# Two token pairs of the first unit turned by VectorE and block transfers instead of TensorE, and three score groups placed behind value products

## The chip, the cores and the metric

One Trainium2 chip, one core. The metric is the device time of one execution in microseconds (us). The core's five engines each work through their own list in program order: PE (TensorE, matrix products), DVE (VectorE), ACT (ScalarE), POOL (GpSimd) and SP (SyncE, which here only issues DMA transfers). An instruction whose inputs aren't ready holds up all that stands behind it on its engine.

## The reference

For 8 batches, 8 heads, 576 tokens and a head width of 64, attention runs within chunks of 64 tokens; its output, with the heads side by side, is 4,608 tokens of 512 features. A normalised two-layer network with 2,048 hidden features follows, and its input is added back.

```
scores = scale * np.matmul(q_c, k_c.transpose(0, 1, 2, 4, 3))
attn = np.exp(scores - np.max(scores, axis=-1, keepdims=True))
attn = attn / (np.sum(attn, axis=-1, keepdims=True) + 1e-09)
x = np.matmul(attn, v_c)
...
xn = (x - mu) / np.sqrt(var + 1e-06) * g_ln
return x + np.maximum(xn @ w_ch1, 0.0) @ w_ch2
```

All of it is in float32 and close to exact: for the two layers each number is split into a high and a low part.

## The kernel before, in words

The 4,608 tokens are 18 pairs of 256 tokens ("pair" in the code), two pairs to a tile. The first three tiles (the lead, pairs 0 to 5) go through the two layers directly: `ffn`, with the products into the hidden features on L589 ("up") and those out of them on L613 ("down"), twelve 128x512 products each, three for each term because of the high and low parts. The other six tiles are three units of two tiles (pairs 6 to 9 are unit 0), whose two layers are computed by a recursive scheme with fewer products (`unit_ffn`, L1109, and `double`, L1039). That scheme needs the normalised tokens with features on the partitions, in a tile `rows`, which `combine` reads (L826 scales, L811 casts, L815 low parts, L818 differences).

`attention` is a generator for one pair: each `yield` ends a step. Its steps for a pair of unit 0 are: load queries and keys (`qk`, L294); the scores (L326); maxima (L333) and the load of the values (`v_t`, L344); subtraction (L359); exponential (L362); turning the probabilities, on PE (L376) or by DVE (L398, 16 instructions); sums; value products (L427); normalisation by the sums (L453 or L461); statistics (L471 to L480) and a copy of the pair to HBM (L274); a pause; the normalised tokens `xg` (L493, two on ACT); and last the tokens are turned so that features lie on partitions. In unit 0 that last part is, for the pairs 6, 8 and 9, eight PE transposes with the identity (L521) in two steps, each with an ACT copy (L522) into `rows`, and for pair 7 sixteen DVE transposes (L529). For pairs 10 and later ("moved") it is one DVE instruction, which turns all 32x32 blocks in place (L500), and then sixteen DMAs of 32 KB in four steps that carry the blocks to their partitions (L508).

The order of the work around here is written by hand. While tiles 1 and 2 go through `ffn`, the tables `SECOND` and `THIRD` say for each token of the `ffn`'s list which streams take a step ahead of it. The letters used below: A and B are pairs 4 and 5, C is pair 6, G is pair 7, D is pair 8, H is pair 9, P is `combine(0, 0)` (of pairs 6 and 8), and S is `prepare`. `prepare` makes weights for the units: POOL sums (L700 to L711), an ACT cast into the tile `parts` (L720), a POOL difference into the same tile (L722), and DMAs to HBM: `w2d` (L705), the four of `parts` (L713, issued one round later) and three of `wa` (L714 to L716). `parts` has one buffer, so the cast of a round waits until the four L713 transfers of the round before have landed. `a`, `b`, T, U and V are `mix` streams (L1077, L1084, ACT cast L1088, L1091, DMA L1093). ACT also makes the hidden features (L602), whose low part is made by DVE (L603).

All DMAs named here but the weights' accumulating ones are issued by SP, in program order, and their completion is counted on eight semaphores in turn, so that a DMA isn't issued before the one eight places ahead of it has landed.

Of the kernel before, what the change touches and what calls it, by code (L numbers as in the profile page):

```python
# [17 lines left out]
P = 128  # L18
B, H, S, D = 8, 8, 576, 64
# [7 lines left out]
NK = DM // P  # L27
# [8 lines left out]
LEAD = 3  # L36
UNITS = (NTILE - LEAD) // 2

SECOND = {
    0: "ABS", 1: "AS", 2: "S", 3: "AAS", 4: "AS", 5: "AS", 6: "AS", 7: "AS", 8: "AAS", 9: "AAS", 10: "AAS", 11: "BAS",  # L40
    12: "BACS", 13: "BS", 14: "S", 15: "BBS", 16: "BS", 17: "BS", 18: "BS", 19: "BS", 20: "BBCS", 21: "BBS", 22: "BBDS",
    23: "BCS", 24: "BCS", 25: "CS", 26: "S", 27: "CCS", 28: "CS", 29: "CCS", 30: "CDS", 31: "CDDS", 32: "DS",
}
THIRD = {
    0: "CS", 1: "CS", 2: "DDGS", 3: "DSaaaaa", 4: "aaaDDS", 5: "DS", 6: "DGS", 7: "GGHSbb", 8: "DGbb", 9: "Db",
    10: "bbTTGGP", 11: "TTHGGPb", 12: "G", 13: "GT", 14: "TTGGHPUU", 15: "GHPTUU", 16: "GHP", 17: "UGP",
    18: "UUHHGPVV", 19: "UHGPVV", 20: "HGPc", 21: "HHPV", 22: "HPVV", 23: "Vd", 24: "ccH", 25: "ccH", 26: "cQQ",
    27: "ccQR", 28: "cQ", 29: "QXXN", 30: "QQR", 31: "Q",
}
# [16 lines left out]
SINGLE = 6  # L66

BY_PE = 2

BY_DMA = (2, 3, 4, 5, 6, 7, 8, 9, 10)  # L70

# [30 lines left out]
def quad(i):  # L102
    return slice(32 * i, 32 * i + 32)
# [3 lines left out]
def chunk_attention_ffn(ctx: ExitStack, tc: tile.TileContext, qkv, v01, g, g_col, w, out):  # L107
# [34 lines left out]
    def weights(f):  # L142
        if f not in wp:
            wp[f] = const.tile([P, 2, NW], F32R, name="wp", tag=f"w{f}")
        return wp[f][:, 0, :], wp[f][:, 1, :]
# [59 lines left out]
    def split_w(i):  # L205
        wf = stage.pop(i)
        f, cs = part(i)
        wh, wl = (x[:, cs] for x in weights(f))
        if i < BY_PE:
            for j in range(wf.shape[1] // HALF):  # L210
# [70 lines left out]
    def attention(pair, xt_cols, xs, by_pe, den_by_pe, rows_of=None, pt_raw=False, pt_by_pe=False):  # L281

        moved = pair >= 2 * LEAD + 4
# [36 lines left out]
        for j in range(2):  # L320
            for a in range(HP):
                for h2 in range(2):
                    r = slice(h2 * D, (h2 + 1) * D)
                    for c in range(2):
                        cs = slice(j * P + c * D, j * P + (c + 1) * D)
# [46 lines left out]
        if by_pe:  # L372
            pt = halves()
            for a in range(groups):
                cs = slice(a % HP * P, (a % HP + 1) * P)
# [6 lines left out]
        elif pt_by_pe:  # L382
            pt = halves()
            for a in range(groups):
                cs = slice(a % HP * P, (a % HP + 1) * P)
# [34 lines left out]
        for j in range(2):  # L420
            for a in range(HP):
                for h2 in range(2):
                    r = slice(h2 * D, (h2 + 1) * D)
                    ja = j * HP + a
                    for c in range(2):
                        cs = slice(c * D, (c + 1) * D)
# [68 lines left out]
                )  # L495
            yield

        if rows_of and moved:
            turned = keep.tile([P, 4, 2 * NK, 32], F32, name="x")
            nc.vector.transpose(  # L500
                out=turned.rearrange("p b a t -> p a b t"),
                in_=xg.rearrange("p j (k b f) -> p (j k) b f", k=NK, b=4),
            )
            yield
            rows_t = rows_of().rearrange("p j k t -> p (j k t)").rearrange("p (j i n) -> p j i n", j=2, i=4)
            for i in range(4):
                for b in range(4):
                    nc.sync.dma_start(  # L508
                        rows_t[quad(b), :, i], turned[quad(i), b].rearrange("p (j k) t -> p j (k t)", j=2)
                    )  # L510
                yield
            return
# [260 lines left out]
    def start_ring():  # L773
        t_ = const.tile([P, 2, 2 * DM], F32R, name="ring", tag="w7")
        ring.add(t_[:, 0], t_[:, 1])
        yield
        for c in "hl":
            t_ = xtp.tile([P, 2, 2 * DM], F32R, name="ring", tag=f"xt{c}")
            ring.add(t_[:, 0], t_[:, 1])
        yield  # L780

    shared = {}

    def rows_of(i):
        if "rows" not in shared:
            shared["rows"] = [xtp.tile([P, 2, 2, NK, P], F32, name="rows", tag=f"xt{c}") for c in "hl"]
        return shared["rows"][i // 2][:, i % 2]

    def operand(name):
        if name not in shared:  # L790
            shared[name] = const.tile([P, 2, 2, 2 * PAIR], F32R, name="xc", tag=f"w{'3621457'.index(name)}")
        return shared[name]

    def combine(u, half=None):
        cs = slice(0, 2 * PAIR) if u > 0 else slice(half * PAIR, (half + 1) * PAIR)
        if u > 0:
            a, b = (
                r.rearrange("p i j k t -> p (i j k t)").rearrange("p (j k t) -> p k j t", k=NK, t=32)
                for r in shared["rows"]
            )  # L800
        else:
            a, b = (r[:, half].rearrange("p j k t -> p k j t") for r in shared["rows"])
        b11, b21, b12, b22 = a[:, :2], a[:, 2:], b[:, :2], b[:, 2:]

        def place(name):
            return operand(name)[:, :, :, cs].rearrange("p h k (j t) -> p h k j t", t=32 if u > 0 else P)

        engine = nc.vector if u > 0 else nc.gpsimd

        def cast(name, x):  # L810
            nc.scalar.copy(place(name)[:, 0], x)  # L811

        def low(name, x):
            o = place(name)
            engine.tensor_tensor(out=o[:, 1], in0=x, in1=o[:, 0].bitcast(F32), op=ALU.subtract)  # L815

        def less(out, x, y):
            nc.vector.tensor_tensor(out=out, in0=x, in1=y, op=ALU.subtract)  # L818

        def part(name, x):  # L820
            cast(name, x)
            low(name, x)

        def gain(x, first):
            for k in range(2):
                nc.scalar.activation(x[:, k], x[:, k], AF.Copy, scale=g_k[:, first + k : first + k + 1])  # L826

        if u > 0:
            steps = [
                [(gain, b21, 2), (gain, b11, 0)], [(cast, "2", b21), (gain, b12, 0)],  # L830
                [(low, "2", b21), (cast, "1", b11), (gain, b22, 2)], [(low, "1", b11), (cast, "3", b22)],
                [(less, b11, b12, b11)], [(low, "3", b22)], [(less, b12, b22, b12)], [(less, b22, b22, b11)],
                [(cast, "6", b22), (cast, "5", b11)], [(low, "6", b22)], [(less, b21, b21, b22)],
                [(low, "5", b11)], [(cast, "7", b12), (cast, "4", b21)], [(low, "7", b12)], [(low, "4", b21)],
            ]
        else:
            steps = [
                [(gain, b21, 2), (part, "2", b21), (gain, b11, 0)], [(part, "1", b11), (gain, b12, 0), (gain, b22, 2)],
                [(less, b11, b12, b11)], [(less, b12, b22, b12)],
                [(part, "3", b22)], [(less, b22, b22, b11)], [(part, "6", b22)], [(part, "5", b11)],  # L840
                [(less, b21, b21, b22)], [(part, "7", b12)], [(part, "4", b21)],
            ]
        for step in steps:
            for what, *args in step:
                what(*args)
            yield
# [219 lines left out]
    def mix(p, engine, pool, tag, again=False):  # L1066
        both = pool.tile([P, 2, 2, DM], F32, name="mixed", tag=tag)
        his, t_ = ([both[:, i, k] for k in range(2)] for i in range(2))
        if again:
            blocks = [[his[k], t_[k]] for k in range(2)]  # L1070
            for k in range(2):
                nc.sync.dma_start(both[:, :, k], w2d[2 * p + k])
            yield
        else:
            blocks = [[x[:, DM:].bitcast(F32) for x in weights(2 * p + k)] for k in range(2)]
        for k in range(2):
            engine.tensor_tensor(out=t_[k], in0=blocks[k][0], in1=blocks[k][1], op=ALU.add)  # L1077
            yield
        b11, b12, b21, b22 = (t_[k // 2][:, k % 2 * PAIR : (k % 2 + 1) * PAIR] for k in range(4))
        for k, (out, x, y, op) in enumerate((  # L1080
            (b11, b12, b11, ALU.subtract), (b12, b22, b12, ALU.subtract), (b22, b11, b22, ALU.subtract),
            (b21, b21, b22, ALU.add),
        )):
            engine.tensor_tensor(out=out, in0=x, in1=y, op=op)  # L1084
            if k % 2:
                yield
        for k in range(2):
            nc.scalar.copy(his[k].bitcast(F32R), t_[k])  # L1088
        yield
        for k in range(2):  # L1090
            engine.tensor_tensor(out=t_[k].bitcast(F32R), in0=t_[k], in1=his[k], op=ALU.subtract)  # L1091
            yield
        nc.sync.dma_start(wb[:, p], both.rearrange("p h k (a n) -> p h (k a) n", a=2))  # L1093
        yield
# [152 lines left out]
    with tc.manual_schedule():  # L1247
# [4 lines left out]
            G=tiles[3].attention(1), H=tiles[4].attention(1, True, pt_raw=True), S=prepare(), R=start_ring(), T=mix(4, nc.gpsimd, const, "w4"),  # L1252
            U=mix(5, nc.gpsimd, raws, "raw"), V=mix(6, nc.gpsimd, const, "w8"), a=mix(1, nc.vector, const, "w0"),
            b=mix(2, nc.gpsimd, const, "w1"), c=mix(0, nc.vector, const, "w9", True), d=mix(3, nc.gpsimd, const, "w10", True),
# [69 lines left out]
```

## Time and profile before

| | us |
|---|---|
| three runs, median (lowest, highest) | 819.19 (818.3, 820.9) |
| the profiled execution | 818.67 |
| its span, first to last instruction | 816.9 |
| PE busy in the span | 806.0 (99%) |
| DVE, ACT, POOL busy | 609.6, 363.1, 183.0 |

The profile is one execution. Its span begins with the first instruction of the program and ends with the last; 1.8 us of the execution's time lie around it. A row of the timeline gives the start, the length, the engine, the line, the operation, what it writes and reads, how many instructions are merged in it, and in brackets the idle time before it with what ended it. Consecutive products overlap in PE's pipeline, so what a group costs is read from the starts: from its first start to the first start of the next group. "SPq" is SP issuing a DMA; the length is that of the issue, not of the transfer. The answer for a line or a tile ends with the time from issue to landing.

### The profile page before, as it was taken

To read this page: it belongs to the slowest core of one execution; us is meant where nothing else is said; L and a number is where in the kernel's file an instruction comes from. 1 tells how busy PE (TensorE), PEld (TensorE's weight loads), DVE (VectorE), ACT (ScalarE), POOL (GpSimd) and SP (SyncE) were. 2 spreads that over 40 slices of the span, in tenths; PEclk is the share of its full clock that TensorE was granted. 3 is DMA by queue.
4 is the path that set the end of the run, shared out by engine and by line. 5 is a ranking of instruction groups with operands and counts; after the bars stand their busy time and mean duration, and the time that the engine had idled before them with its cause. 6 is when DMAs were issued, how large, how long until landed. Compare 5 with 4: busy or idle time off the path is not lost.

```text
span 816.9 us, 15499 instructions
## 1 busy us (share of the span) xinstructions
PE 806.0 (99%) x6170; PEld 680.3 (83%) x6170; DVE 609.6 (75%) x885; ACT 363.1 (44%) x545; POOL 183.0 (22%) x199
## 2 busy tenths in 40 slices
PE   7999999999999999999999999999999999999998
PEld 4888888888888888888888898888888988888887
DVE  6999975787665876869789987697799922249974
ACT  4776432121335434344567442443675522345450
POOL 0111005653857975610100001300000040000000
PEclk9999999999999999999999999999999999999999
DMA  9998315967786239988789578877796678668663
GB/s 359 331 291 243 156 52 183 364 201 253 272 307 252 104 129 367 368 300 302 250 248 329 184 236 307 278 276 257 239 334 213 183 236 252 186 203 285 193 214 108
DMA packets 113928, 201.06 MB, mean 246 GB/s; under 512 B 8512, under 2 KB 75072, under 8 KB 109888
## 3 DMA queue, kind: packets, MB, share of 16 engines
q1 hardware_dynamic: 112560, 195.35, 70.2%
q0 software_dynamic: 1296, 4.72, 3.0%
q8 instruction: 49, 0.80, 0.4%
q14 instruction: 23, 0.19, 0.1%
HBM read 142.89 MB, written 48.23 MB: 234 GB/s over the span
## 4 chain that ended last, share of the span: by engine, by line
PE 98%; DMA 1%; DVE 0%; issue 0%; SPq 0%; ACT 0%
PE y L1109 28%; PE h L589 16%; PE y L613 16%; PE y L1039 12%; PE h L1039 10%; PE s L1039 7%; PE s L326 2%; PE h L427 1%; DMA qk<-qkv 1%; PE s L427 1%; PE s L376 1%; PE s L353 0%; PE s L386 0%; PE y L251 0%; PE s L521 0%; PE y L542 0%
## 5 line engine op out<-in xcount | busy, mean ns | idle before, releaser
L1109 PE MATMUL y<-xc,ring 128*128 128x512 f32 x1008 | 233.4, 391 | 0.0
L1109 PEld LDWEIGHTS y<-xc,ring 128*128 128x128 f32 x1008 | 188.0, 188 | 39.5 <-issue 0.4
L613 PE MATMUL y<-wp,hidden 128*128 128x512 f32 x564 | 137.8, 393 | 0.0
L589 PE MATMUL h<-xth,wp 128*128 128x512 f32 (+1 forms) x432 | 129.6, 371 | 0.0
L613 PEld LDWEIGHTS y<-wp,hidden 128*128 128x128 f32 x564 | 104.4, 188 | 21.4
L1118 DVE TENSOR_TENSOR hu<-y,snap 128x512 f32<-128x512 f32 x72 | 49.2, 685 | 78.7 <-ACT snap L1115 38.3
L589 PEld LDWEIGHTS h<-xth,wp 128*128 128x128 f32 x432 | 78.2, 188 | 14.6 <-DVE hidden L603 0.6
L1039 PE MATMUL y<-ring,hx 128*128 128x512 f32 (+1 forms) x448 | 79.8, 337 | 0.0
L1115 ACT COPY snap<-y 128x512 f32<-128x512 f32 x72 | 41.8, 587 | 83.9 <-PE y L1109 83.8
L935 ACT ACTIVATE hx<-hu 128x1024 fp32r<-128x1024 f32 x61 | 64.3, 1061 | 33.0 <-PE h L1039 24.3
L589 PE MATMUL h<-xtl,wp 128*128 128x512 f32 (+1 forms) x216 | 78.3, 367 | 0.0
L1039 PEld LDWEIGHTS y<-ring,hx 128*128 128x128 f32 x448 | 69.6, 190 | 9.4
L603 DVE SCALAR_TENSOR_TENSOR hidden<-h,hidden 128x512 fp32r<-128x512 f32 (+1 forms) x53 | 33.0, 629 | 54.2 <-ACT hidden L602 54.0
L1039 PE MATMUL h<-ring,hx 128*128 128x256 f32 (+1 forms) x332 | 71.5, 319 | 0.0
L602 ACT ACTIVATE hidden<-h 128x512 fp32r<-128x512 f32 (+1 forms) x53 | 28.5, 545 | 95.5 <-PE h L589 95.5
L944 DVE TENSOR_TENSOR hx<-hu,hx 128x1024 fp32r<-128x1024 f32 x51 | 62.4, 1223 | 7.9 <-ACT hx L935 7.8
L1039 PE MATMUL s<-ring,hx 128*128 128x256 f32 (+1 forms) x236 | 59.7, 335 | 0.0
L997 POOL TENSOR_TENSOR x<-parts,x 128x512 f32<-128x512 f32 x16 | 20.3, 1290 | 169.4 <-DVE x L964 169.0
L1039 PEld LDWEIGHTS h<-ring,hx 128*128 128x128 f32 x332 | 52.0, 190 | 4.8
L398 DVE STREAM_TRANSPOSE pt_sb<-p_sb 32x256 f32<-32x256 f32 x112 | 48.8, 436 | 4.3 <-ACT p_sb L362 2.3
L589 PEld LDWEIGHTS h<-xtl,wp 128*128 128x128 f32 x216 | 40.2, 188 | 6.6 <-ACT xtl L552 0.2
L1039 PEld LDWEIGHTS s<-ring,hx 128*128 128x128 f32 x236 | 40.6, 190 | 4.8
(177 smaller groups left out, 1153.4 us busy)
## 6 DMA issues: line engine op xcount, KB each, us to landing
ring<-wa SPq DMA_DIRECT2D x84, 512.0 KB, 4.6
ring<-wb SPq DMA_DIRECT2D x48, 512.0 KB, 3.7
ring<-w2d SPq DMA_DIRECT2D x36, 512.0 KB, 4.5
raw<-w SPq DMA_DIRECT2D x15, 1024.0 KB, 7.9
out<-x SPq DMA_DIRECT2D x22, 512.0 KB, 5.4
qk<-qkv SPq DMA_DIRECT2D x18, 512.0 KB, 6.4
w2d<-wp SPq DMA_DIRECT2D x16, 512.0 KB, 6.8
wa<-parts SPq DMA_DIRECT2D x32, 256.0 KB, 4.6
```

The source lines that it names most:

```text
L398: nc.vector.transpose(out=pt_sb[quad(2 * h2 + j), :, c, quad(i)], in_=p_sb[quad(2 * c + i), :, h2, quad(j)])
L589: nc.tensor.matmul(h, lhsT=(wh, wh, wl)[m][:, ks], rhs=(xth, xtl, xth)[m][:, k, :], start=i == 0, stop=i == len(terms) - 1,)
L602: nc.scalar.activation(hh, h, AF.Relu)
L603: nc.vector.scalar_tensor_tensor(out=hl, in0=h, scalar=0.0, in1=hh.bitcast(F32), op0=ALU.max, op1=ALU.subtract)
L613: nc.tensor.matmul(sums(pairs[j // 2])[j % 2], lhsT=(hh, hh, hl)[m], rhs=(wh, wl, wh)[m], start=f == 0 and m == 0, stop=f == NF - 1 and m ...
L935: nc.scalar.activation(hh, self.split[k][2], AF.Relu if x == "1" else AF.Copy)
L944: nc.vector.tensor_tensor(out=hl, in0=x, in1=hh.bitcast(F32), op=ALU.subtract)
L997: engine.tensor_tensor(out=x, in0=self.staged[at][:, 2 * i : 2 * i + 2], in1=x, op=ALU.add)
L1039: nc.tensor.matmul(y, lhsT=(hh, hh, hl, hh)[m], rhs=w.rearrange("p h n -> p (h n)") if m == BOTH else w[:, (0, 1, 0)[m]], start=p == 0 and ...
L1109: nc.tensor.matmul(bank, lhsT=w[:, (0, 0, 1)[m], ks], rhs=x[:, (0, 1, 0)[m], k, :], start=start and k == m == 0, stop=k == 1 and m == 2, s ...
L1115: nc.scalar.copy(out, bank)
L1118: nc.vector.tensor_tensor(out=out, in0=bank, in1=s, op=ALU.add)
```

## The change

In `attention`, the pairs 6 and 8 (`BY_BLOCKS`) take the way of the later pairs: one DVE instruction and sixteen DMAs in place of eight PE transposes and two ACT copies. `combine(0, 0)` reads `rows` with 32-token blocks, the layout that the DMAs write. In the tables, the streams C and D have three steps more (17 in place of 14), C's last five at the end of `SECOND` and in `THIRD` 0 and 1, D's in `THIRD` 7 and 8; P's second step moves from `THIRD` 11 to 13. Besides, the score steps of pairs 5, 6 and 9 move: B's from `SECOND` 11 to 7, C's from 20 to 19 and H's from `THIRD` 11 to 13, each directly behind the step with another pair's value products.

```
 SECOND = {
...
-    12: "BACS", 13: "BS", 14: "S", 15: "BBS", 16: "BS", 17: "BS", 18: "BS", 19: "BS", 20: "BBCS", 21: "BBS", 22: "BBDS",
+    12: "BACS", 13: "BS", 14: "S", 15: "BBS", 16: "BS", 17: "BS", 18: "BS", 19: "BCS", 20: "BBS", 21: "BBS", 22: "BBDS",
...
 THIRD = {
...
-    10: "bbTTGGP", 11: "TTHGGPb", 12: "G", 13: "GT", 14: "TTGGHPUU", 15: "GHPTUU", 16: "GHP", 17: "UGP",
+    10: "bbTTGGP", 11: "TTGGb", 12: "G", 13: "GHTP", 14: "TTGGHPUU", 15: "GHPTUU", 16: "GHP", 17: "UGP",
...
+BY_BLOCKS = (2 * LEAD, 2 * LEAD + 2)
...
-        if rows_of and moved:
+        if rows_of and (moved or pair in BY_BLOCKS):
             turned = keep.tile([P, 4, 2 * NK, 32], F32, name="x")
             nc.vector.transpose(
...
-        if u > 0:
-            a, b = (
-                r.rearrange("p i j k t -> p (i j k t)").rearrange("p (j k t) -> p k j t", k=NK, t=32)
-                for r in shared["rows"]
-            )
-        else:
-            a, b = (r[:, half].rearrange("p j k t -> p k j t") for r in shared["rows"])
+        wide = 32 if u > 0 or half == 0 else P
+        a, b = (
+            (r if u > 0 else r[:, half : half + 1]).rearrange("p i j k t -> p (i j k t)").rearrange(
+                "p (j k t) -> p k j t", k=NK, t=wide
+            ) for r in shared["rows"]
+        )
```

In the changed file the lines of `attention` stand two further down (L508 is L510, L294 is L296), those of `prepare` too (L713 is L715, L720 is L722), and those behind `combine` one further.

**SP, the boundary of tiles 1 and 2.** Before, the four output DMAs of tile 1 (L636) are followed by the queries and keys of pair 7 (L294), and then by a round of `prepare`:

```order
L636 DMA out<-x 128x512 x4
L294 DMA qk<-qkv 128x1024 x2
L705 DMA w2d<-wp 128x2x512 x2
L713 DMA wa<-parts 128x2x256 x4
L714 DMA wa<-wp 128x2x256
L715 DMA wa<-wp 128x2x256
L716 DMA wa<-wp 128x2x256
```

Now, with pair 6's sixteen block DMAs (`rows<-x`), and further down the first eight of pair 8's:

```order
L638 DMA out<-x 128x512 x4
L510 DMA rows<-x 32x2x128 x16
L296 DMA qk<-qkv 128x1024 x2
L707 DMA w2d<-wp 128x2x512 x2
L715 DMA wa<-parts 128x2x256 x4
L716 DMA wa<-wp 128x2x256
L717 DMA wa<-wp 128x2x256
L718 DMA wa<-wp 128x2x256
L1094 DMA wb<-mixed 128x2048
L276 DMA out<-x 128x2x512
L510 DMA rows<-x 32x2x128 x8
```

The sixteen stand ahead of the queries and keys, of `w2d` and of the four DMAs of `parts`.

**ACT, a little later.** Before, from the `mix` cast of stream a over the last cast of `parts` (L720) to the `mix` cast of stream b:

```order
L1088 CAST mixed<-mixed 128x512 x2
L602 ACTIVATE hidden<-h 128x512
L720 CAST parts<-sums 128x1024
L602 ACTIVATE hidden<-h 128x512
L493 ACTIVATE xg<-x,vare,rstd 128x512 x2
L602 ACTIVATE hidden<-h 128x512
L522 COPY rows<-s 128x512
L362 ACTIVATE p_sb<-p_sb 128x1024
L522 COPY rows<-s 128x512
L1088 CAST mixed<-mixed 128x512 x2
L602 ACTIVATE hidden<-h 128x512
```

Now:

```order
L1089 CAST mixed<-mixed 128x512 x2
L604 ACTIVATE hidden<-h 128x512
L722 CAST parts<-sums 128x1024
L604 ACTIVATE hidden<-h 128x512
L495 ACTIVATE xg<-x,vare,rstd 128x512 x2
L604 ACTIVATE hidden<-h 128x512
L364 ACTIVATE p_sb<-p_sb 128x1024
L1089 CAST mixed<-mixed 128x512 x2
L604 ACTIVATE hidden<-h 128x512
```

The two copies of pair 8 are gone; the cast of `parts` has kept its place ahead of two hidden activations, of pair 8's `xg` and of stream b's cast.

**PE, the value products of pair 7 (L427, `h<-v_t,pt_sb`).** Before, a down group stands on either side of them:

```order
L613 MATMUL y<-wp,hidden 128x512 x12
L427 MATMUL h<-v_t,pt_sb 64x64 x32
L613 MATMUL y<-wp,hidden 128x512 x12
L589 MATMUL h<-xth,wp 128x512
L589 MATMUL h<-xtl,wp 128x512
```

Now the scores of pair 9 (`s<-qk`) stand right behind them; before they stood by themselves, one down and one up group earlier:

```order
L615 MATMUL y<-wp,hidden 128x512 x12
L429 MATMUL h<-v_t,pt_sb 64x64 x32
L328 MATMUL s<-qk 64x64 x32
L615 MATMUL y<-wp,hidden 128x512 x12
L591 MATMUL h<-xth,wp 128x512
```

The scores of pairs 5 and 6 move in the same way, behind the value products of pairs 4 and 5.

More of the change, by code (lines that the diff above doesn't have):

```diff
@@ L39 @@
 SECOND = {
-    0: "ABS", 1: "AS", 2: "S", 3: "AAS", 4: "AS", 5: "AS", 6: "AS", 7: "AS", 8: "AAS", 9: "AAS", 10: "AAS", 11: "BAS",
-    12: "BACS", 13: "BS", 14: "S", 15: "BBS", 16: "BS", 17: "BS", 18: "BS", 19: "BS", 20: "BBCS", 21: "BBS", 22: "BBDS",
-    23: "BCS", 24: "BCS", 25: "CS", 26: "S", 27: "CCS", 28: "CS", 29: "CCS", 30: "CDS", 31: "CDDS", 32: "DS",
+    0: "ABS", 1: "AS", 2: "S", 3: "AAS", 4: "AS", 5: "AS", 6: "AS", 7: "ABS", 8: "AAS", 9: "AAS", 10: "AAS", 11: "AS",
+    12: "BACS", 13: "BS", 14: "S", 15: "BBS", 16: "BS", 17: "BS", 18: "BS", 19: "BCS", 20: "BBS", 21: "BBS", 22: "BBDS",
+    23: "BCS", 24: "BCS", 25: "CS", 26: "S", 27: "CCS", 28: "CS", 29: "CCS", 30: "CDS", 31: "CDDS", 32: "CDS",
 }
 THIRD = {
-    0: "CS", 1: "CS", 2: "DDGS", 3: "DSaaaaa", 4: "aaaDDS", 5: "DS", 6: "DGS", 7: "GGHSbb", 8: "DGbb", 9: "Db",
-    10: "bbTTGGP", 11: "TTHGGPb", 12: "G", 13: "GT", 14: "TTGGHPUU", 15: "GHPTUU", 16: "GHP", 17: "UGP",
+    0: "CCS", 1: "CCS", 2: "DDGS", 3: "DSaaaaa", 4: "aaaDDS", 5: "DS", 6: "DGS", 7: "DDDGGHSbb", 8: "DDGbb", 9: "b",
+    10: "bbTTGGP", 11: "TTGGb", 12: "G", 13: "GHTP", 14: "TTGGHPUU", 15: "GHPTUU", 16: "GHP", 17: "UGP",
     18: "UUHHGPVV", 19: "UHGPVV", 20: "HGPc", 21: "HHPV", 22: "HPVV", 23: "Vd", 24: "ccH", 25: "ccH", 26: "cQQ",
@@ L795, in combine @@
         cs = slice(0, 2 * PAIR) if u > 0 else slice(half * PAIR, (half + 1) * PAIR)
-        if u > 0:
-            a, b = (
-                r.rearrange("p i j k t -> p (i j k t)").rearrange("p (j k t) -> p k j t", k=NK, t=32)
-                for r in shared["rows"]
-            )
-        else:
-            a, b = (r[:, half].rearrange("p j k t -> p k j t") for r in shared["rows"])
+        wide = 32 if u > 0 or half == 0 else P
[4 more added lines that the diff above has]
+        )
         b11, b21, b12, b22 = a[:, :2], a[:, 2:], b[:, :2], b[:, 2:]
         def place(name):
-            return operand(name)[:, :, :, cs].rearrange("p h k (j t) -> p h k j t", t=32 if u > 0 else P)
+            return operand(name)[:, :, :, cs].rearrange("p h k (j t) -> p h k j t", t=wide)
         engine = nc.vector if u > 0 else nc.gpsimd
```

## The prediction

> **What bounds the kernel now.** First the page: the engines' busy time, and the chain of work that ended last by engine.
>
> ```profile
> PE 806.0 (99%) x6170; PEld 680.3 (83%) x6170; DVE 609.6 (75%) x885; ACT 363.1 (44%) x545; POOL 183.0 (22%) x199
> ...
> PE 98%; DMA 1%; DVE 0%; issue 0%; SPq 0%; ACT 0%
> ```
>
> PE works from end to end, and the chain is PE's own list. Whatever leaves PE's list is saved in full, and whatever makes PE wait is lost in full. So I price the edit on PE first, and then follow the added instructions to the first place where PE could wait for them. The timeline of PE around pair 7's scores and pair 8's transposes:
>
> ```profile
> 240.94 2.88 PE L613 MATMUL y<-wp,hidden 128*128 128x512 f32 x12
> 243.66 0.39 PE L589 MATMUL h<-xth,wp 128*128 128x512 f32 x1
> ...
> 246.47 1.16 PE L326 MATMUL s<-qk 64*64 64x64 f32 x64
> 247.56 3.02 PE L613 MATMUL y<-wp,hidden 128*128 128x512 f32 x12
> 250.42 0.39 PE L589 MATMUL h<-xth,wp 128*128 128x512 f32 x1
> ...
> 253.15 0.60 PE L521 MATMUL s<-ident,xg 128*128 128x128 f32 x4
> 253.50 3.02 PE L613 MATMUL y<-wp,hidden 128*128 128x512 f32 x12
> 256.36 0.60 PE L521 MATMUL s<-ident,xg 128*128 128x128 f32 x4
> ```
>
> A plain group of twelve takes 2.72 from start to start (240.94 to 243.66); ahead of scores it takes 2.81, behind scores or transposes 2.86. There is no idle time in these rows.
>
> **The change part by part: what PE saves.** Four transposes hold PE for 0.35 (253.15 to 253.50) and lengthen the next group by 0.14: 0.49. Four such groups go: 1.96. Scores by themselves cost 1.09 (246.47 to 247.56) + 0.09 + 0.14 = 1.32; value products cost the same. Unit 1 shows the two side by side:
>
> ```profile
> 343.11 1.16 PE L427 MATMUL h<-v_t,pt_sb 64*64 64x64 f32 x64
> 344.09 1.11 PE L326 MATMUL s<-qk 64*64 64x64 f32 x64
> 345.14 12.54 PE L1109 MATMUL y<-xc,ring 128*128 128x512 f32 x54
> ```
>
> Together 2.03 + 0.09 + 0.14 = 2.26 in place of 2.64: 0.38 saved, three times 1.14. PE's list is 3.1 shorter. If nothing made PE wait, the profiled execution would take 818.67 - 3.1 = 815.6.
>
> **What is added ahead of others on SP.** Four block DMAs issued in a row in unit 1, the time from issue to landing of all 128 of them, and SP's list where pair 6's sixteen now go in, behind L636:
>
> ```profile
> 362.70 2.50 SPq L508 DMA_DIRECT2D rows<-x  x4
> DMA to landing us min/median/max: 1.9/3.6/8.0
> 227.22 2.31 SPq L636 DMA_DIRECT2D out<-x  x4
> 229.62 0.90 SPq L294 DMA_DIRECT2D qk<-qkv  x2
> 230.57 0.94 SPq L705 DMA_DIRECT2D w2d<-wp  x2
> ```
>
> Four hold SP for 2.50 and the step to the next, sixteen for about 10.2. L636 ends at 229.53 and follows PE, which by then has saved two of the score groups (0.76), so I put its end at 228.8 and pair 7's L294 at 239.0 in place of 229.6. The trouble isn't L294 (see below) but the four L713 behind it. What waited for them so far, from the answer for the tile `parts`, and the stretch of 229.5 to 239.5 in the table of windows (the last two columns are the DMA engines' share and GB/s):
>
> ```profile
> L720 ACT CAST parts<-sums x8: 1033/1044/1052, 137.8 to 241.9; 128x1024 fp32r<-128x1024 f32 x8
>   DMA wa<-parts: 7.5, 3
> DMA to landing us min/median/max: 2.4/4.6/7.1
> 229.50:239.50 10.00, 10.00 (x110) 8.20 (x109) 5.85 (x8) 3.21 (x6) 8.19 (x7) 1.00 0.99 331
> ```
>
> The cast waited three times, 7.5 in all, for L713 to land. The transfers ran at 0.99 of the engines' time and 331 GB/s; two L294, two L705 and four L713 are 3 MB, so 9.5 at that rate, plus 1.9, the shortest landing of a block DMA: the last L713 lands at 239.0 + 9.5 + 1.9, about 250.4. Upper end: before, the cast that waits for it began at 241.93 (below), 12.3 after L294: 251.3. Lower end: SP needs 0.90 + 0.94 for the first four and as long for four more, so the last is issued at 242.7, and with L713's median of 4.6 lands at 247.3. I take 250.4, since here 2 MB go ahead of the L713 at one time, which the median of all 28 doesn't show.
>
> At one place the Trainium skill would give another sum: "DMA: Bandwidth & Descriptors", section "Issuing engines are not separate DMA queues", says that the time a sequencer takes to start a DMA is usually small beside the DMA. By that rule the sixteen would hardly shift L713 and the sum would stay near 815.6. The trace agrees for large loads (two L294 issued in 0.90, with a median of 6.4 to landing, quoted below) and less for blocks: 0.62 of issue apiece against 1.9 to 3.6, sixteen times over.
>
> **What waits behind the cast.** On ACT, POOL and DVE:
>
> ```profile
> 241.93 1.03 ACT L720 CAST parts<-sums 128x1024 fp32r<-128x1024 f32 x1
> ...
> 248.40 1.52 ACT L493 ACTIVATE xg<-x,vare,rstd 128x512 f32<-128x512 f32 x2 [1.17 <-POOL vare L480]
> ...
> 257.47 1.14 ACT L1088 CAST mixed<-mixed 128x512 fp32r<-128x512 f32 x2
> 259.83 0.60 ACT L602 ACTIVATE hidden<-h 128x512 fp32r<-128x512 f32 x1 [1.22 <-PE h L589]
> 248.36 2.40 POOL L722 TENSOR_TENSOR parts<-sums,parts 128x1024 fp32r<-128x1024 f32 x1
> ...
> 253.21 3.19 POOL L1084 TENSOR_TENSOR mixed<-mixed 128x256 f32<-128x256 f32 x4
> 260.46 0.69 DVE L603 SCALAR_TENSOR_TENSOR hidden<-h,hidden 128x512 fp32r<-128x512 f32 x1 [5.74 <-ACT hidden L602]
> 261.07 7.21 DVE L398 STREAM_TRANSPOSE pt_sb<-p_sb 32x256 f32<-32x256 f32 x16
> ```
>
> Before, POOL came to L722 only at 248.36, so a cast at 241.93 had 5.4 to spare. With the cast at 250.4 it is ACT that POOL waits for: cast 1.05, hand-over 0.1, L722 to the end of L1084 8.04 (248.36 to 256.40), the second L1088 and the hidden activation behind it 0.05 + 0.52 + 0.63 (each starts before its forerunner's row ends), DVE from 260.46 to 268.28 7.82, hand-over 0.1: 18.3. Then pair 7's probabilities are turned and PE can begin its value products: 250.4 + 18.3 = 268.7. The place on PE:
>
> ```profile
> 269.14 1.16 PE L427 MATMUL h<-v_t,pt_sb 64*64 64x64 f32 x64
> 270.24 3.02 PE L613 MATMUL y<-wp,hidden 128*128 128x512 f32 x12
> ```
>
> Without a wait PE would be there at 269.14 - 0.76 - 1.96 - 1.32 (pair 9's scores now come after it) = 265.1. So it waits 3.6, in one piece or partly earlier: a hidden activation stands behind the held cast too and ends at 250.4 + 1.05 + 0.6 = 252.1, while PE wants it for the down group of 253.50, now at 253.50 - 0.76 - 3 x 0.49 = 251.3; these 0.8 are contained in the 3.6. At the next down group PE starts at 268.7 + 2.03 = 270.7, where it was at 270.24 before. Sum: 3.1 saved, 3.6 waited, 0.5 lost: 818.67 + 0.5 = 819.2. The profiled execution lies 0.5 below the median of the three runs, 819.19, which gives 819.7 by it; I say 819.5, between the two. With the landing at 251.3 it is 1.4 lost, at 249.9 nothing, below 246.8 the 3.1 are kept.
>
> **Edits at no cost.** The two DVE transposes of 1.24 each, DVE's idle time where they fall, and a later hidden activation on ACT:
>
> ```profile
> L500 DVE STREAM_TRANSPOSE x<-xg x8: 1235/1240/1246, 354.2 to 577.1; 128x1024 f32<-128x1024 f32 x8
> 226.44 2.73 DVE L631 SCALAR_TENSOR_TENSOR x<-y,rstd,x 128x512 f32<-128x512 f32 x4 [2.24 <-POOL sums L708]
> 254.03 0.69 DVE L603 SCALAR_TENSOR_TENSOR hidden<-h,hidden 128x512 fp32r<-128x512 f32 x1 [3.68 <-ACT hidden L602]
> 276.01 0.60 ACT L602 ACTIVATE hidden<-h 128x512 fp32r<-128x512 f32 x1 [5.88 <-PE h L589]
> ```
>
> They fall into idle time of 2.24 and 3.68; without it each would put 1.24 on DVE's list. ACT loses four copies; the scaling in `combine` has as many elements as before. Pair 7's queries and keys: issued at 239.0 to 239.9, with a median of 6.4 to landing (row below) they are there at 246.3, and PE wants them at 246.47 - 0.76 - 0.98 = 244.7. That wait, up to 1.6, lies inside the 3.6; it counts only where the later wait is gone. P's second step waits on ACT for pair 8's blocks. SP issues the second eight in 5.0 behind pair 9's L294 (263 at the latest, below) and four L729 (2.25), so they land, 1.9 to 3.6 later, at 272 to 274; the next hidden activation, for which PE would wait, stood at 276.01: covered by 2.
>
> **The rivals.** *Covers hold (faster).* The last L713 lands by 247.3 or sooner, the lower end. For it: the queues empty while SP issues blocks of 32 KB, and the shortest landing of L713 is 2.4. Against: 3 MB must still pass. At 247.3 PE waits 247.3 + 18.3 - 265.1 = 0.5, so 816.1; at 246.8 or less 815.6, plus a possible wait for pair 7's keys. I put it at 815.9. The Trainium skill's rule above would lead here.
>
> *Pair 9's keys late (slower).* The held cast also holds pair 8's L493, so pair 8's transpose ends at 252.1 + 1.5 + 1.24, near 254.8, and its first eight blocks leave SP at 259.8; behind them stand the values of pair 7 (L344), pair 9's L294 and the last four `parts` (L729); the third row is L294's time to landing:
>
> ```profile
> 245.59 2.41 SPq L344 DMA_DIRECT2D v_t<-qkv  x2
> ...
> 250.79 2.25 SPq L729 DMA_DIRECT2D wa<-parts  x4
> DMA to landing us min/median/max: 3.5/6.4/9.3
> ```
>
> L294 ends near 262 to 263 (with 1.2 to 2.4 for L344). PE wants pair 9's scores at 268.7 + 1.0 = 269.7; the median lands at 268.4 to 269.4, the maximum at 272. From 269.7 on each us is lost on top: with 2.3 the total is 2.8 lost, 821.5. Against it: with the median PE still has 0.3 to 1.3 in hand.
>
> **How the numbers follow.** A difference of 0.3%, 2.46, is about what a measurement can tell from none. Forecast, a loss between -0.9 and 1.6: 0.63, all within 0.3%. Covers hold: 0.23, of which 0.17 gain over 2.46 and 0.06 less. Pair 9's keys late, or both ends at once: 0.14, of which 0.13 over 2.46. Faster 0.17, same 0.70, slower 0.13. The range goes from 816.1, which leaves out about 0.1 of the full gain, to 821.5.
>
> **What would show it.** Right: in the changed profile the last ACT cast of `parts` (L722) waits for DMA `wa<-parts` and starts near 250; POOL's L724 waits for ACT; DVE's sixteen L400 end near 268.6; PE is idle for 3 to 4 between 250 and 269, most of it ahead of L429, released by DVE. Of L521's 24 transposes only pair 9's eight are left (as L523), and the three score groups cost 0.38 less each. Wrong: if PE shows no idle time there, the covers held and the time is near 815.6; if the idle time stands before L328 and ends with DMA `qk<-qkv`, the keys of pair 9 (or 7) were what came late.

## The result, and the profile after

| | before | after |
|---|---|---|
| median of five runs each (lowest, highest), us | 819.45 (818.3, 820.9) | 823.19 (822.53, 824.70) |
| the profiled execution, us | 818.67 | 823.19 |
| its span, us | 816.9 | 821.4 |

The ratio on record is 1.0054, with a 95% interval of 1.0040 to 1.0067. It is estimated from the runs and isn't the quotient of the two medians, which lie 3.7 apart (1.0046). By either the change is slower, and its time lies above the forecast's range of 816.1 to 821.5.

The page of the changed kernel: busy time of the engines, the granted TensorE clock in 40 slices, and the chain that ended last.

```profile
PE 806.3 (98%) x6154; PEld 681.4 (83%) x6154; DVE 612.8 (75%) x887; ACT 360.8 (44%) x541; POOL 182.7 (22%) x199
...
PEclk9999999999999899999999999999999999999999
...
PE 89%; DVE 4%; DMA 3%; SPq 2%; issue 1%; ACT 0%; ACTq 0%; DVEq 0%
```

PE has 16 instructions fewer and yet is busy for 0.3 more. In one slice the clock is below full, and DVE, DMA and SP have entered a chain of which PE had 98%. PE's waits (total, times, longest):

```profile
PE h L429 <- DVE hidden L605: 3.2, 1, 3.2
...
PE h L591 <- DMA wp<-wfs: 1.3, 1, 1.3
PE s L328 <- DVE mv L474: 1.2, 1, 1.2
```

The 1.3 for the weights `wfs` falls at 54 us, before anything that was changed. The profiled runs differ there from one execution to the next (before's had no such wait, an experiment's below one of 2.6), so the changed profile runs 1.21 late from the start. I subtract that in what follows. The 1.2 ahead of pair 7's scores (L328) is put down to DVE, but it is the wait for pair 7's keys: the experiment that loads them earlier (keys first, below) takes it away, and two other kernels have a wait of 1.6 and 1.7 at this place that ends with DMA `qk<-qkv`. SP, and what stood behind it on ACT, POOL and DVE:

```profile
230.06 10.81 SPq L510 DMA_DIRECT2D rows<-x  x16
240.97 1.00 SPq L296 DMA_DIRECT2D qk<-qkv  x2
...
243.06 3.82 SPq L715 DMA_DIRECT2D wa<-parts  x4
```

```profile
252.35 1.05 ACT L722 CAST parts<-sums 128x1024 fp32r<-128x1024 f32 x1 [10.10 <-DMA wa<-parts]
...
276.86 1.71 ACT L827 ACTIVATE rows<-rows,mhalf 128x256 f32<-128x256 f32 x4 [4.80 <-DMA rows<-x]
```

```profile
253.48 2.41 POOL L724 TENSOR_TENSOR parts<-sums,parts 128x1024 fp32r<-128x1024 f32 x1 [4.89 <-ACT parts L722]
```

```profile
262.73 0.69 DVE L605 SCALAR_TENSOR_TENSOR hidden<-h,hidden 128x512 fp32r<-128x512 f32 x1 [3.19 <-ACT hidden L604]
263.34 7.21 DVE L400 STREAM_TRANSPOSE pt_sb<-p_sb 32x256 f32<-32x256 f32 x16
270.58 0.69 DVE L605 SCALAR_TENSOR_TENSOR hidden<-h,hidden 128x512 fp32r<-128x512 f32 x1
```

The brackets spell the forecast's chain: the sixteen blocks, the load of `parts`, the cast held for 10.10, POOL behind ACT, DVE behind ACT. PE at the end of it, and the clock there (in the table of windows the number behind POOL is the granted clock):

```profile
247.15 1.16 PE L328 MATMUL s<-qk 64*64 64x64 f32 x64 [1.17 <-DVE mv L474]
...
267.77 0.33 PE L429 MATMUL h<-v_t,pt_sb 64*64 64x64 f32 x4
271.32 1.87 PE L429 MATMUL h<-v_t,pt_sb 64*64 64x64 f32 x58 [3.22 <-DVE hidden L605]
...
274.93 3.90 PE L615 MATMUL y<-wp,hidden 128*128 128x512 f32 x12
278.67 0.40 PE L591 MATMUL h<-xth,wp 128*128 128x512 f32 x1
```

```profile
268.20:270.00 1.80, 0.00 (x0) 0.00 (x0) 1.75 (x5) 0.62 (x1) 1.64 (x3) 0.99 0.94 327
270.00:276.80 6.80, 5.47 (x128) 4.98 (x129) 6.49 (x12) 1.14 (x2) 4.55 (x5) 0.50 0.60 203
276.80:280.00 3.20, 3.20 (x15) 2.62 (x14) 1.95 (x4) 1.71 (x4) 2.71 (x4) 1.00 1.00 367
```

Four products find their operands (the first half of the turned probabilities); the fifth waits. And there is what the forecast hadn't: the clock falls to one half at 270.0, while PE stands still, and stays there for 6.8. Value products and scores then take 3.61 (271.32 to 274.93), where an experiment below takes 2.01 at full clock, and the down group 3.74 instead of 2.86: 2.48 lost. The up group behind starts at 278.67, 5.58 later than in the kernel before:

```profile
273.09 0.39 PE L589 MATMUL h<-xth,wp 128*128 128x512 f32 x1
```

Without the 1.21 of the start that is 4.37. About 1.06 comes back later, 0.75 of which is an interruption of PE at 511 us that before's profile has and this one hasn't (last section): 1.21 + 4.37 - 1.06 = 4.52, the difference of the two profiled executions.

### The profile page after: what moved, and what is told of

The parts are those of the page before. It is cut to its first block, busy times and chain, and to the rows that moved or that the text cites. A ratio compares the mean times of both kernels' runs of the same rounds, so it can differ in the third digit from the quotient of the medians.

```text
span 821.4 us, 15513 instructions
## 1 busy us (share of the span) xinstructions
PE 806.3 (98%) x6154; PEld 681.4 (83%) x6154; DVE 612.8 (75%) x887; ACT 360.8 (44%) x541; POOL 182.7 (22%) x199
## 4 chain that ended last, share of the span: by engine, by line
PE 89%; DVE 4%; DMA 3%; SPq 2%; issue 1%; ACT 0%; ACTq 0%; DVEq 0%
PE y L1110 28%; PE y L615 13%; PE h L591 13%; PE y L1040 12%; PE h L1040 10%; PE s L1040 7%; PE s L328 2%; SPq L510 2%; PE h L429 2%; DMA wp<-wfs 1%; DVE pt_sb L400 1%; DMA qk<-qkv 1%; DMA wa<-parts 1%; PE s L429 0%; PE s L355 0%
```

## The experiments

The theory, **held cast**: the sixteen blocks at the head of SP's list hold the cast, the chain behind it ends after PE needs it, and PE's clock falls in the wait. The rival, **blocks or scores themselves**: pair 8's late blocks, DVE's extra transposes, the traffic, or the moved scores. Ratios are to the kernel before, with 95% intervals.

### Which part costs: e1, e4, e3, e2

**Scores only**: the kernel before, with the new places of B, C and H in the tables.

> The kernel before with the three score groups moved and nothing else; the tokens of pairs 6 and 8 stay on PE. Theory (held cast: the sixteen block DMAs of pair 6 on SP hold the load of pair 7's keys and the cast of parts, and with it pair 7's value products; PE's clock falls in the wait): none of this can happen here, so three times 0.38 are saved, 1.1 less than before (ratio 0.9986), and PE does not wait ahead of pair 7's value products. Rival (the moved scores are at fault: pair 9's scores now stand behind the late value products of pair 7 and keep the hidden activation back): 1 to 4 slower than before. The share of the transposes in the saving is then what the other kernels save beyond 1.1.

Measured 1.0003 (0.9994 to 1.0012): no loss, but the priced 1.1 isn't there. PE and DVE of this kernel:

```profile
267.97 0.33 PE L427 MATMUL h<-v_t,pt_sb 64*64 64x64 f32 x4
269.20 1.09 PE L427 MATMUL h<-v_t,pt_sb 64*64 64x64 f32 x58 [0.90 <-DVE hidden L603]
...
271.21 3.02 PE L613 MATMUL y<-wp,hidden 128*128 128x512 f32 x12
```

```profile
261.21 7.21 DVE L398 STREAM_TRANSPOSE pt_sb<-p_sb 32x256 f32<-32x256 f32 x16
268.45 0.69 DVE L603 SCALAR_TENSOR_TENSOR hidden<-h,hidden 128x512 fp32r<-128x512 f32 x1
```

PE waits ahead of the same products with no cast held (`parts` is cast at 242.43). DVE's sixteen transposes start behind the hidden part of an up group of PE, and PE goes on 0.06 after the end of the next hidden part. In the kernel before, DVE was through with that at 269.01 and PE came at 269.14, with 0.1 of slack:

```profile
268.32 0.69 DVE L603 SCALAR_TENSOR_TENSOR hidden<-h,hidden 128x512 fp32r<-128x512 f32 x1
```

So pair 9's scores, taken out of just this stretch, save nothing there, and they now stand behind the wait. The other two groups have saved 0.77 by 241 us; the move of pair 9's loses 0.83, so that the down group behind starts 0.06 later than before (both without the 0.91 by which this execution started late). This is a second limit that neither theory had.

**Pair 6 only by blocks** (`BY_BLOCKS = (2 * LEAD,)`, D's steps as before, with pair 8's ACT copies writing the 32-token layout).

> Only pair 6 by blocks, pair 8 turned by PE, the scores moved. Theory (held cast): the sixteen stand where they stood in the change, so the cast starts near 251 and the loss stays: the change's ratio of 1.0054 plus the 0.98 of pair 8's transposes that is not saved, about 1.006 to 1.007; PE waits 3 ahead of pair 7's value products. Rival (pair 8's blocks): 2.1 less than before, ratio 0.9974.

Measured 1.0056 (1.0042 to 1.0069), as the theory has it, though at another place:

```profile
255.28 1.22 DVE L361 TENSOR_TENSOR p_sb<-s,top 128x1024 f32<-128x1024 f32 x1
256.64 0.80 PE L523 MATMUL s<-ident,xg 128*128 128x128 f32 x4 [3.20 <-DVE p_sb L361]
257.10 4.54 PE L621 MATMUL y<-wp,hidden 128*128 128x512 f32 x12
```

With pair 8 back on PE, its first transposes come ahead of the value products. The tokens they turn (L495) are ready at 254.79; the wait ends with DVE's subtraction of pair 7's scores, which stands behind a hidden part on DVE (253.42) that waits for ACT's hidden activation behind the held cast (251.84). That the transposes write to the place from which the subtraction reads (both are `s`) would explain the wait, but no run here tests it. PE waits 3.2, and the group behind takes 4.37 in place of 2.86, most of it at half clock; at the value products only the 0.9 of the kernel above is left.

**Pair 8 only by blocks** (`BY_BLOCKS = (2 * LEAD + 2,)`, C's steps as before, with pair 6's ACT copies writing the 32-token layout).

> Only pair 8 by blocks, pair 6 turned by PE as before the change (with its two copies written into the 32-token layout), the scores moved. Theory (pair 6's sixteen at the head of SP's list are the cause): no hold, 0.98 of transposes and 1.14 of scores saved, 2.1 less than before, ratio 0.9974. Rival (pair 8's blocks, which land at 276.6 in the changed kernel and keep ACT's scaling L827 waiting for 4.8, are the cause): as slow as the change, or, with the first wait gone, 2 to 3 lost there.

Measured 0.9979 (0.9970 to 0.9987): faster, so pair 8's blocks aren't the cause. The priced 2.1 lie inside this interval. In the trace the down group behind the scores starts 0.94 earlier than before (without the 0.87 of a late start), and what is missing of the 2.1 by then is the same wait for DVE, 0.9, with the four early products, 0.33.

**All blocks, pair 6's behind the loads of `parts`**:

```
-    0: "CCS", 1: "CCS", 2: "DDGS", 3: "DSaaaaa", 4: "aaaDDS", ...
+    0: "S", 1: "S", 2: "DDGS", 3: "DSCCaaaaa", 4: "CCaaaDDS", ...
```

> The changed kernel with pair 6's sixteen block DMAs issued a few tokens later, behind the four L715 and the three L716 to L718, all else the same. Theory (held cast): pair 7's keys and parts land as early as before, the cast of parts starts near 241 instead of 252.35, PE waits neither for the keys nor ahead of pair 7's value products, its clock stays at 1.0, and the whole 3.1 is saved: ratio near 0.996, 816.3. Rival (the block route itself costs: late blocks of pair 8, two more transposes on DVE, 32 transfers of 32 KB beside the other loads): still as slow as the change, ratio 1.004 to 1.007. In between, 0.997 to 1.002: a second wait of 1 to 3 stood hidden behind the first, and the trace will show its place.

Measured 0.9977 (0.9965 to 0.9990). The order of SP's list alone turns the ratio of 1.0054 into 0.9977, a loss into a gain of 1.9. The cast starts at 242.91, and PE shows what is left:

```profile
267.64 1.15 PE L429 MATMUL h<-v_t,pt_sb 64*64 64x64 f32 x60 [0.90 <-DVE hidden L605]
269.62 1.16 PE L328 MATMUL s<-qk 64*64 64x64 f32 x64 [0.83 <-DMA qk<-qkv]
```

The wait for DVE again, and 0.83 for pair 9's keys: the prediction's second rival, in small, once the larger wait is gone.

### Issue, threshold, containment: e8, e6, e12

**Transfers only**: the kernel before and, at pair 6's place on SP, sixteen DMAs more of its tokens `xg`, 32 KB each, to a scratch.

> The kernel before with sixteen block DMAs of 32 KB more at the place where the change has pair 6's, from the normalised tokens of pair 6 to a scratch in HBM that nobody reads; tokens stay on PE, scores where they were, no DVE transpose is added. Theory (the issue of the sixteen on SP is the cause): the last of the parts DMAs lands near 251.5 instead of 241.9, the cast starts there, and the chain of 19 behind it ends at 270.5, so PE waits about 1.4 ahead of pair 7's value products, which it reached at 269.14: ratio 1.0017, up to 1.004 if the clock falls as well. Rival (not the transfers but DVE's work and the moved scores): no wait, ratio 1.000.

Measured 1.0077 (1.0062 to 1.0091). No transpose is saved or added and no score moved, and the loss is there, larger than I expected. ACT and PE:

```profile
252.96 1.05 ACT L727 CAST parts<-sums 128x1024 fp32r<-128x1024 f32 x1 [10.04 <-DMA wa<-parts]
```

```profile
257.77 1.08 PE L528 MATMUL s<-ident,xg 128*128 128x128 f32 x4 [3.19 <-DVE p_sb L359]
258.50 5.38 PE L620 MATMUL y<-wp,hidden 128*128 128x512 f32 x12
```

The cast is held as expected; my place was wrong, as for pair 6 alone: pair 8's transposes come first, and wait for the same subtraction on DVE. The down group behind takes 5.22 from start to start in place of 2.86, at a clock of 0.5 for 6.8. This kernel adds issue and traffic at once. SP is held for 10.87 by the sixteen; their 0.5 MB alone would take 1.6 at the 331 GB/s of this stretch in the kernel before (an estimate), so most of the hold is issue.

**Half ahead**: eight blocks stay, eight go behind L718 (`THIRD` 0 "CCS", 1 "S", 3 "DSCCaaaaa").

> The changed kernel with eight of pair 6's sixteen blocks left where they are, the other eight behind L715 to L718. Theory (held cast, with a threshold): eight fewer DMAs ahead bring the last L715 down about 5.1 earlier, to 247, the cast starts there, and the chain of 19 behind it ends at 266.3, before PE comes; pair 7's keys land at 242. What is left is what the kernel with all sixteen behind shows: ratio near 0.998. Rival (each block ahead costs its share): half the way between 0.998 and 1.0054, about 1.0015.

Measured 0.9969 (0.9957 to 0.9980), as with all sixteen behind:

```profile
247.06 1.05 ACT L722 CAST parts<-sums 128x1024 fp32r<-128x1024 f32 x1 [5.99 <-DMA wa<-parts]
```

A cast held for 6 costs nothing: there is a threshold between eight and sixteen blocks, not a price per block.

**Keys first** (`THIRD` 0 "GCCS", 2 "DDS").

> The changed kernel with pair 7's queries and keys (two DMAs) ahead of pair 6's sixteen blocks, all else the same. It takes away the wait of 1.2 ahead of pair 7's scores. If that wait lies inside the later one, as the prediction had it, PE comes to the value products 1.2 earlier, waits about 4.5 there and starts again at the same time: ratio as the change, 1.004 to 1.007. If the waits add up, 1.2 are gained: ratio 1.0039, and the wait at the value products stays 3.2.

Measured 1.0027 (1.0014 to 1.0041). PE:

```profile
254.37 3.03 PE L615 MATMUL y<-wp,hidden 128*128 128x512 f32 x12 [1.62 <-ACT hidden L604]
...
271.72 1.87 PE L429 MATMUL h<-v_t,pt_sb 64*64 64x64 f32 x58 [3.19 <-DVE hidden L605]
...
274.99 3.04 PE L615 MATMUL y<-wp,hidden 128*128 128x512 f32 x12
```

The 1.2 ahead of pair 7's scores is gone, a wait for the hidden activation behind the held cast has come (1.62), and the value products restart 18.95 after the cast's start, as in the change (18.97). So in the trace the earlier waits lie inside the later one, as predicted. The clock is one half for about 3.4 here (1 us windows from 271: 0.56, 0.50, 0.50, 0.74), and the products and scores take 3.27, the down group its full-clock time. That costs 1.26 instead of 2.48 and makes the difference of the two profiled executions. It doesn't explain the ratio, which is 0.0027 under the change's and below the 1.004 that I expected: the mean clock on record is 0.996 in two of the change's five executions and in five of the twelve here, and 0.998 in the others, so both lengths seem to occur in both kernels in like shares (an estimate: 6.8 us at half clock lower the mean by 0.4%, 3.4 us by 0.2%). The two intervals touch. Whether the 0.0027 is noise or a gain stays open, and so does why the half clock is 3.4 long in one execution and 6.8 in another.

### The clock: e7, e5

**PE kept busy**: ahead of pair 7's value products

```
...
+            for i in range(14):
+                nc.tensor.matmul(z[:, i % 2, :], lhsT=minus, rhs=wide_, start=True, stop=True)
```

> The changed kernel with 14 products of 128x512 more on PE right ahead of pair 7's value products; their result is used by nobody. They add about 3.2 of work to PE's list, just where PE stood idle for 3.2. If the halved clock behind the wait (scores and value products and the next down group, 3.2 longer than priced at most) comes from PE's standing still, PE keeps its full clock here and the kernel is 2 to 2.5 faster than the change although it does more: ratio to before about 1.0025. If the clock has another cause, or the clock's fall costs nothing, the ratio stays at 1.0054 or rises.

Measured 1.0035 (1.0023 to 1.0047): 0.0019 or 1.6 less than the change, with more work; the intervals overlap, so the time alone doesn't show it. The trace does. PE:

```profile
268.86 3.34 PE L415 MATMUL s<-minus 128*128 128x512 f32 x14
...
274.48 3.01 PE L620 MATMUL y<-wp,hidden 128*128 128x512 f32 x12
277.33 0.39 PE L596 MATMUL h<-xth,wp 128*128 128x512 f32 x1
```

The clock stays at 1.00 in every 1 us window from 256 to 280. From the end of DVE's hidden part (272.41) to the up group it is 4.92, in the change 7.40 (271.27 to 278.67): 2.48 again. Of the whole execution less than 2 to 2.5 came, since the cast was later here (253.51, in before's time 1.7 later than in the change) and the interruption of PE is there again (0.8). Without their different starts the two profiled executions are equally long.

**Values later** (13 "TP", 14 "GHTTGGHPUU").

> The changed kernel with pair 7's value products and pair 9's scores one token of the ffn's list later, after the next down and up group. SP's list, the late cast of parts and the chain behind it stay. Theory (held cast): PE comes to the value products at about 273.4, two after the turned probabilities are there, so the wait of 3.2 and the halved clock behind it are gone; left are 3.1 saved, the wait for pair 7's keys (1.2) and 0.1 for the hidden activation: 1.7 less than before, ratio 0.998. If pair 8's blocks (landed at 276.6) now hold the hidden activation that stands behind ACT's scaling, about 2 of it go and the ratio is 1.000. Rival (the loss does not come from this wait but from the blocks' traffic or DVE's added transposes): as slow as the change, 1.004 to 1.007.

Measured 1.0008 (0.9996 to 1.0020), the upper of my two cases, but not by pair 8's blocks. PE's waits:

```profile
PE y L615 <- DVE hidden L605: 1.6, 1, 1.6
...
PE y L615 <- ACT hidden L604: 1.3, 1, 1.3
PE s L328 <- DVE mv L474: 1.2, 1, 1.2
```

The wait moved into the down group, which needs the hidden part that DVE makes behind the sixteen transposes. Three waits of 1.2 to 1.6 leave the clock at 1.00. The profiled execution is the longest of twelve (823.14; their median is 819.34), and it has one more wait, for the weights `wfs` near the start:

```profile
50.29 0.56 PE L591 MATMUL h<-xth,wp 128*128 128x256 f32 x2 [2.56 <-DMA wp<-wfs]
```

From 50.6 to 54.0 the clock is 0.50: PE's standing still for 2.56 was enough too.

### The stretch through DVE: e10, e13, e9

**Turned earlier**: the scores only, and `THIRD` 9 "DGGb", 11 "TTPb", so that eight of the sixteen transposes go ahead of the hidden part.

> The kernel with the scores moved and the tokens on PE (ratio 1.0003 instead of the priced 0.9986), and besides eight of the sixteen DVE transposes of pair 7's probabilities one token earlier. Theory (the stretch from an up group over ACT's and DVE's hidden, sixteen transposes and one more DVE hidden to the value products is 9.2 long and leaves PE no slack, so the 1.3 taken off PE's list inside this stretch are waited for): without that loop PE does not wait at L427 and the priced 1.1 appear, ratio 0.9986. Rival (the moved scores save nothing by themselves): ratio stays at 1.0003.

Measured 0.9979 (0.9968 to 0.9991). DVE and PE:

```profile
256.30 3.57 DVE L398 STREAM_TRANSPOSE pt_sb<-p_sb 32x256 f32<-32x256 f32 x8 [2.34 <-PE s L521]
...
260.62 3.60 DVE L398 STREAM_TRANSPOSE pt_sb<-p_sb 32x256 f32<-32x256 f32 x8
```

```profile
267.06 1.16 PE L427 MATMUL h<-v_t,pt_sb 64*64 64x64 f32 x64
```

No wait: the down group behind starts at 269.08, 1.16 before the kernel before. The price of the scores (1.14) was right, and the stretch through DVE took it.

**Hold kept**: the change, with 7 "HDDDGGSbb", 9 "GGb", 11 "TTb".

> The changed kernel with pair 6's sixteen blocks left ahead, so that the cast of parts is held as before, but with eight of the sixteen DVE transposes of pair 7's probabilities one token earlier and pair 9's keys ahead of pair 8's blocks (the two other edits of the kernel that reached 0.994). Theory (the loss is the held cast in series with sixteen transposes): the chain behind the cast is 3.6 shorter, ends near 267.7, and PE, which comes at 267.8, does not wait at the value products; the clock stays at 1.0; left is the wait for pair 7's keys (1.2) and 0.1 to 1.3 for a hidden activation: ratio 0.996 to 0.998. If the hold itself is enough for the loss, the ratio stays above 1.002.

Measured 0.9992 (0.9981 to 1.0003), less than expected:

```profile
PE s L328 <- DMA qk<-qkv: 1.7, 1, 1.7
PE y L615 <- ACT hidden L604: 1.3, 1, 1.3
PE h L429 <- DVE hidden L605: 0.7, 1, 0.7
```

The cast is held longer here than in the change (12.04, start 254.10), and yet no wait reaches 2 and the clock stays full. The hold isn't free, though: the next kernel, which differs from this one only in where pair 6's blocks stand, has 0.9941, so the hold costs 0.0051 here, in three short waits, against 0.0077 without the two edits (1.0054 and 0.9977). What sixteen transposes in series add to it is the one long wait and the half clock.

**Covers restored**: these two edits, and pair 6's blocks behind the loads of `parts`.

> The changed kernel with pair 6's sixteen blocks behind the DMAs of parts, eight of the sixteen DVE transposes of pair 7's probabilities one token earlier, and pair 9's keys ahead of pair 8's blocks. It takes away the three waits that the trace of the kernel with the blocks behind (0.9977) still shows: 0.9 idle and 0.33 of four early products ahead of the value products, released by DVE, and 0.8 for pair 9's keys. If these waits are what is missing of the 3.1, the ratio is 0.996, near 816.2. If something else takes the place, for instance pair 8's blocks ahead of ACT's scaling, the ratio stays near 0.9977.

Measured 0.9941 (0.9929 to 0.9954), 814.46: the fastest of all. After 60 us PE waits for nothing:

```profile
265.08 1.16 PE L429 MATMUL h<-v_t,pt_sb 64*64 64x64 f32 x64
266.06 1.11 PE L328 MATMUL s<-qk 64*64 64x64 f32 x64
267.11 3.02 PE L615 MATMUL y<-wp,hidden 128*128 128x512 f32 x12
```

267.11 against 270.24: 3.13, the 3.1 of the sum. Pair 8's blocks again keep ACT waiting (4.04) at no cost. The medians are 4.9 apart, more than I expected. Of the other 1.7, none of it priced, 0.75 is the missing interruption at 511 us, 0.33 comes between 531 and 552 (its cause isn't settled), and 0.7 is that before's profiled execution lies so much under its median here (819.33).

## Why the prediction was wrong, step by step

The chain was foreseen link by link, and it is the one that the trace shows; two terms of its sum were too small and one was missing. In before's time (the changed profile less 1.21):

| step | predicted | measured |
|---|---|---|
| PE's list | 3.1 shorter | 3.13 (covers restored) |
| last load of `parts` landed | 250.4 | 251.1, near the upper end |
| landing to restart of the value products | 18.3 | 19.0 |
| PE there without the earlier wait | 265.1 | 265.4 (267.77 - 1.21 - 1.17) |
| clock behind the wait | not in the sum | 2.48 |

**What failed first is the sum's last line**, "At the next down group PE starts at 268.7 + 2.03": it priced what follows a wait at the speed of the trace of before, in which PE never stood still and the clock was 1.00 throughout. The wait halved the clock. The Trainium skill, "TensorE: Matmul & The Clock Gate", Part 1, says that the clock is halved after at least one idle window of some 3.4 us, and comes back after as long a busy one. The trace agrees on the halving and on lengths in multiples of 3.4, not on the idle time: here a wait of 3.2 was enough, and the clock fell 1.9 after PE had stopped; in another kernel 2.56 was enough (values later). With this term alone the forecast would have been about 822, outside its range; the other two terms below, 1.4 together, would have left it at 820.9, inside.

**The chain of 18.3** ended with a hand-over of 0.1 behind the last transpose. PE goes on 0.77 behind it (270.55 to 271.32), 0.05 behind the DVE instruction that follows. In all runs this instruction follows at once, so whether PE waits for its end or the transposes' results are late by as much isn't told apart. **The landing** came 0.7 late: sixteen blocks held SP for 10.91 (230.06 to 240.97), not 10.2. With the forecast's 0.5 these make 0.5 + 0.7 + 0.7 + 2.5 = 4.4, as measured (4.37).

Of the edits said to cost nothing: the wait for pair 7's keys (1.2) lay inside the later one, as said; pair 9's scores followed the value products without a wait, so the slower rival didn't come about; pair 8's blocks were landed only near 275.6, not 272 to 274, and yet nobody on PE waited for ACT's scaling; the added transposes found room.

**The rival "covers hold"** was wrong in its own right. It had the whole 3.1 with `parts` landed by 246.8. The kernel with the blocks behind lands it before 243 and gets 1.9: the value products wait for DVE, a stretch of 9.2 from ACT's hidden part (258.42 there) to the restart (267.64) that hangs on PE's own up group, and that had 0.1 of slack in the kernel before. I had followed that stretch only behind a held cast, never without one. The Trainium skill's rule behind that rival ("DMA: Bandwidth & Descriptors", "Issuing engines are not separate DMA queues") is not borne out: the transfers alone, put ahead on SP, cost 6.3.

## What to carry to other kernels

Price what you put at the head of a DMA queue by the issue time of all its parts, and follow the first single-buffered tile behind it through every engine; then ask the same of the path that ends second, since the saving stops there. Here single waits of PE of 2.6 and 3.2 us cost more than their length, since the clock fell; split into waits of up to 1.7 or filled with work that nobody needs, they left it alone. Where the gain stays out, look for an order: the same instructions, three edits of the tables apart, took 823.2 and 814.5.

## What the runs showed of the hardware

- Half clock after one wait of 3.2 in four kernels (the change, pair 6 only, transfers only, keys first) and after one of 2.56 in a fifth (values later), for 3.4 or 6.8, beginning 1.9 to 3.5 after PE stopped; in no profile after waits of up to 2.1, apart from the idle 2.4 at the program's start. Where between 2.1 and 2.56 it begins, or whether the length alone decides, stays open.
- The kernel before has a mean clock of 0.997 or 0.998 in five of 35 executions, its five longest (821.6 to 822.3). None of them was profiled, so the place isn't known.
- PE stops for 0.4 to 1.5 within the same group of scores (between 511 and 520 us), ended by "issue", in the profiles of all five kernels with 6,168 or 6,170 PE instructions, and in none of the nine with 6,162 or fewer:

```profile
511.80 0.33 PE L326 MATMUL s<-qk 64*64 64x64 f32 x2 [0.44 <-issue]
```

  The change with 14 products more (PE kept busy) has it again. What is behind it stays open.
